# Two FNet + gated-unit layers on one core: a new hand-written opening, and input tests moved away from layer 2's first down projection

## The chip, the core and the metric

One core of one Trainium2 chip runs the kernel. TensorE (PE) does the matrix products, VectorE (DVE) and ScalarE (ACT) the elementwise work, GpSimd (POOL) small work, and SyncE (SP) issues the loads and stores. The metric is the device time of one execution in microseconds (us).

## The reference

The input x has 2048 rows (sequence) of 640 columns (hidden). Two layers follow, with the same weights, each of two residual steps:

```python
def _A_ref(x, dft_seq_re, dft_seq_im, dft_hid_re, dft_hid_im):
    a = jnp.einsum("bsd,ed->bse", x, dft_hid_re)
    b = jnp.einsum("bsd,ed->bse", x, dft_hid_im)
    return jnp.einsum("ts,bse->bte", dft_seq_re, a) - jnp.einsum("ts,bse->bte", dft_seq_im, b)

def _B_ref(x, w_gate, w_up, w_down):
    h = _sigmoid(x @ w_gate) * (x @ w_up)        # 640 -> 1728
    return h @ w_down                            # 1728 -> 640

for layer in range(2):
    x = x + _A_ref(_layernorm(x), ...)
    x = x + _B_ref(_layernorm(x), ...)
```

All arrays are float32. The four DFT matrices are inputs like the others: 2048 x 2048 for the sequence, 640 x 640 for the hidden dimension, real and imaginary part each.

## The kernel before

**Two programs in one.** `folded` does the work under the assumption that the DFT matrices have the symmetries of a DFT; it folds rows and columns onto each other, so that a quarter of the sequence matrix is enough, and makes the gate, up and down products from seven block products instead of eight. Operands are split into a high and a low float16 part. At the same time it tests on the chip whether the matrices do have those symmetries, and writes the result to `flag`. If they don't, `general` computes everything again in the plain way; on the inputs given it does not run.

**The tests.** There are 100. Each loads a piece of a DFT matrix (`load_rows`, L1490, four loads; `load_hidden_rows`, L1550, two loads that gather single rows; and their like for columns), compares it with its mirror image on VectorE (L1497 and L1499, L1554), and sums the squares of what is left on ScalarE (L1469). Three rooms of memory are used in turn. Test n's load is placed at `at_test(n)`, its compares at `at_test(n + 2)`, its square just after, at `n + 2.85`. All loads stand in SP's queue, together with those that the layers need.

**Order by a plan.** The program is straight-line code, and each engine works off its own queue in the order in which it was written. From the end of the opening on the order comes from a plan: the list of TensorE's steps with estimated durations gives each a place on an axis T of about one unit per us, and `when(t, f)` writes job f at place t of that axis, between the steps. It sets an order only; nothing waits for a clock. `start_of(1, "d", 0)`, here called d0, is the place of layer 2's (layer index 1) first down projection. The tests are spread evenly over a list of stretches with weights, `spans`: a stretch of weight 0.4 has tests at 0.4 of the density of one with weight 1.0, and `pace` is the weighted sum of the lengths divided by 100.

**The down projection.** Layer 2's down runs in seven stages (`stage`, L1418) for each half of the columns. Each stage needs three tables of 320 KB each, which layer 1 had stored in HBM as `kept_f`; `load_stage(s)` (L1366) loads them. Stage 0's are placed at d0 - 16, stage 1's at d0 + 0.5, stage 2's at d0 + 5. The results are taken out of the accumulators by VectorE (L1292). The products ahead of it, gate and up, are `seven` (L1162); ScalarE copies their accumulators out (L1166). Behind the down comes the next gate and up, whose input is turned by a transposing load (L528).

**The opening.** For the first part of layer 1, up to the first gate and up, the order of the jobs is a string written by hand, `OPENING`. A row block i is 512 rows, in four parts A to D of 128. `turn i B` mirrors a part on TensorE (L352), `turned` copies the result out on ScalarE (L358). `stats i A` takes the statistics of a part for the layer norm: on ScalarE (L578, L579) when `(i, GA)` is in `ON_ACT`, on VectorE (L419, L420) otherwise. `col i k` folds columns of two parts (L588, L589, twice VectorE), `double` is L595 on GpSimd, `zero i` clears the columns past the fold (L846, GpSimd). `means`, `smeans`, `power` and `scale` work out the norm's factors (L375, L363, L400/L401, L405 to L409), `re`, `ro`, `de`, `do` scale the folded rows (ScalarE L629 and L631, VectorE L635), `join i e` and `join i o` add them up (L665), and `seq` is the first product on TensorE (L824). `evhi` and `ev` take its result out as a high (L237, ScalarE) and a low part (L239, VectorE). Loads of weights (`wld`) and splits (`whhi`, `wshi` and so on) stand between.

**Memory.** All big buffers are slots of one tile, `big`. Which address a slot gets is read from a long list of numbers, `PLACES`, in the order in which the slots are taken; a changed order needs a new list.

Of the kernel before, what the change touches and what calls it, by code (L numbers as in the profile page):

```python
# [19 lines left out]
D = 640  # L20
# [50 lines left out]
JC = 6  # L71
# [35 lines left out]
311 372 252 359 204 297 350 151 264 212 377 100 226 132 161 118 355"""  # L107
# [20 lines left out]
class Slot:  # L128
# [19 lines left out]
GA, GB, GC, GD = range(4)  # L148
# [13 lines left out]
    smeans 2, means 2, turn 3 C, ro 1 0, join 0 e, ro 1 1, double 1 1, re 1 1, do 0 1, do 1 0, power 2, double 2 0,
    re 1 0, join 0 o, turned 3 C, turned 3 B, do 1 1, stats 3 A, square 3 C, zero 1, square 3 B, de 1 1, scale 2,
    de 1 0, join 1 o, seq 0 1, ro 2 0, row 1, stats 3 D, means 3, re 2 0, join 1 e, col 3 1, col 3 0, double 2 1,
    ro 2 1, smeans 3, seq 0 0, de 2 0, re 2 1, power 3, do 2 0, do 2 1, seq 1 1, de 2 1, double 3 0, seq 1 0,
    double 3 1, evhi 0 1 2, ev 0 1 2, wshi 1 0, whhi 1, scale 3, evhi 0 1 1, ro 3 1, join 2 e, join 2 o, wld 4 1,
    re 3 1, evhi 0 1 0, re 3 0, whhi 3, de 3 1, do 3 1, ro 3 0, de 3 0, seq 2 0, do 3 0, whhi 4, join 3 e, join 3 o,
    ev 0 1 1, evhi 0 0 0, wld 5 0, evhi 0 0 2, whhi 2, zero 3, whhi 5, seq 3 0, ev 0 0 0, whlo 5, wshi 3 0,
    evhi 1 0 0, evhi 0 0 1, whhi 0, ev 1 0 0, wld 3 1, seq 2 1, evhi 1 0 1, ev 0 0 2, ev 0 0 1, wshi 2 1, whlo 1,
    whlo 3, whlo 0, whlo 2, wshi 4 1, wshi 1 1, whlo 4, ev 1 0 1, wshi 0 0, hid 0 0, evhi 1 0 2, ev 1 0 2, wslo 1 1,  # L170
    hid 0 1, wslo 2 1, difhi 0, ev 0 1 0, difhi 1, wslo 3 0, dif 0, dif 1, seq 3 1, evhi 1 1 1, hid 1 1, wshi 0 1,
# [8 lines left out]
ON_ACT = {(0, GA), (2, GA), (2, GD), (3, GA), (3, GD)}  # L180
# [22 lines left out]
def folded(ctx, tc, pool, dram, big, acc, flag, x, ct, wh, wg, wu, wc, wd, out):  # L203
# [1509 lines left out]
    def start_of(*key):  # L1713
        return T[marks[key]]
# [83 lines left out]
    for layer in range(2):  # L1798
# [343 lines left out]
```

## Time and profile before

| | us |
|---|---|
| median of 3 runs | 1116.61 |
| the three runs | 1118.42, 1116.54, 1116.61 |
| profiled execution, its own time | 1118.15 |
| its span, first to last instruction | 1116.3 |
| mean granted TensorE clock | 0.992 |
| TensorE busy | 1090.2 (98%) |
| VectorE busy | 827.8 (74%) |
| ScalarE busy | 570.8 (51%) |
| GpSimd busy | 157.6 (14%) |

Rows of the profile that stand below come in four forms. A row of the order of time has the start in us, the duration in us, the engine, the line of the program, the operation, what it writes and reads, and how often it came in a row; in square brackets stands how long the engine sat idle before it and what ended that. "SPq" is SyncE issuing a load. A row of the waits has the engine and its line, what it waited for, and us in total, times and longest. A row of the windows gives busy time by engine and the granted clock (PEclk, 1.00 is full), the DMA share and GB/s. "big<-kept_f" means that `big` is written from `kept_f`; in the windows (x72) is a count of instructions.

### The profile page before, as it was taken

The numbers are of one execution on the slowest core, as the hardware profiler recorded it, in microseconds if no ns is written. First come the engines' busy times: TensorE is split into PE (matmuls) and PEld (weight loads), VectorE is DVE, ScalarE is ACT, GpSimd is POOL, SyncE is SP. The second block draws the span as 40 slices with busy tenths as digits, with TensorE's granted clock in tenths as the row PEclk, the third lists the DMA queues.
The fourth block names the chain that finished last, engine by engine and source line by source line (L and its number), as shares of the span: only waits on it lengthen the run. The fifth ranks groups of instructions, "written<-read, shape, count | busy, mean of one in ns | idle before, by whom it ended". The sixth has DMA issues, their size and how long they took to land.

```text
span 1116.3 us, 17439 instructions
## 1 busy us (share of the span) xinstructions
PE 1090.2 (98%) x6279; PEld 620.7 (56%) x6279; DVE 827.8 (74%) x1608; ACT 570.8 (51%) x1108; POOL 157.6 (14%) x245
## 2 busy tenths in 40 slices
PE   5999999999999999999999999999999999999997
PEld 3667444447774444457776844444567444444775
DVE  7986679857548999769786559876797356767962
ACT  7765447765334656455234534575554245454520
POOL 3110143321324143000100100002000010000010
PEclk8899999999999999999999999999999999999999
DMA  8414674365888789656733049635669875665621
GB/s 272 151 37 106 180 208 170 100 214 153 206 232 274 252 228 281 212 171 218 220 90 112 1 88 169 208 120 188 200 150 196 219 228 188 207 207 175 201 84 63
DMA packets 183081, 194.70 MB, mean 174 GB/s; under 512 B 76459, under 2 KB 145476, under 8 KB 182984
## 3 DMA queue, kind: packets, MB, share of 16 engines
q1 hardware_dynamic: 182344, 190.86, 58.4%
q0 software_dynamic: 640, 2.62, 0.6%
q8 instruction: 51, 0.84, 0.3%
q14 instruction: 46, 0.38, 0.1%
HBM read 145.29 MB, written 31.90 MB: 159 GB/s over the span
## 4 chain that ended last, share of the span: by engine, by line
PE 86%; DVE 7%; DMA 5%; ACT 1%; issue 1%; SPq 0%; DVEq 0%; POOL 0%; ACTq 0%; POOLq 0%
PE acc L1162 37%; PE acc L1418 14%; PE acc L1118 14%; PE acc L1304 8%; PE acc L912 4%; DMA big<-in_ct 2%; PE acc L824 2%; PE acc L1399 2%; PE acc L1271 2%; PE acc L781 1%; DMA big<-big 1%; DMA big<-in_x 1%; DVE big L1292 1%; DVE big L239 1%; DVE big L1379 0%
## 5 line engine op out<-in xcount | busy, mean ns | idle before, releaser
L1162 PE MATMUL acc<-big 128*128 128x512 f16 x2160 | 467.8, 379 | 2.8 <-DMA big<-big 1.1
L1162 PEld LDWEIGHTS <-big 128*128 128x128 f16 x2160 | 211.2, 98 | 258.1 <-issue 3.0
L1418 PE MATMUL acc<-big 128*128 128x320 f16 x1512 | 214.0, 299 | 5.1 <-DVE big L1292 2.5
L1418 PEld LDWEIGHTS <-big 128*128 128x128 f16 x1512 | 147.8, 98 | 64.3 <-issue 4.0
L1166 ACT ACTIVATE big<-acc 128x512 f32<-128x512 f32 x160 | 93.8, 592 | 168.6 <-PE acc L1162 168.2
L1118 PE MATMUL acc<-big 128*128 128x512 f16 (+1 forms) x900 | 156.3, 336 | 0.0
L1118 PEld LDWEIGHTS <-big 128*128 128x128 f16 x900 | 87.9, 98 | 67.6 <-issue 0.3
L1469 ACT ACTIVATE big<-big 128x768 f32<-128x768 f32 (+6 forms) x106 | 79.1, 746 | 85.2 <-DVE big L1499 43.9
L239 DVE SCALAR_TENSOR_TENSOR big<-big 128x640 f16<-128x640 f32 (+8 forms) x94 | 75.8, 831 | 22.6 <-POOL big L1072 11.4
L1304 PE MATMUL acc<-big 128*128 128x320 f16 x656 | 89.3, 299 | 0.0
L1292 DVE SCALAR_TENSOR_TENSOR big<-acc,big 128x320 f32<-128x320 f32 x112 | 53.0, 484 | 47.6 <-PE acc L1399 27.3
L1379 DVE TENSOR_TENSOR big<-big 128x512 f16<-128x512 f32 x126 | 84.5, 681 | 4.5 <-ACT big L1378 4.4
L237 ACT ACTIVATE big<-big 128x640 f16<-128x640 f32 (+9 forms) x94 | 63.6, 708 | 43.2 <-DMA big<-in_ct 19.6
L1378 ACT ACTIVATE big<-big 128x512 f16<-128x512 f32 x126 | 72.6, 616 | 18.6 <-DVE big L1379 7.0
L1304 PEld LDWEIGHTS <-big 128*128 128x128 f16 x656 | 64.2, 98 | 25.1
L1212 DVE TENSOR_TENSOR big<-big,acc 128x512 f32<-128x512 f32 x40 | 27.2, 681 | 42.6 <-PE acc L1162 32.0
L1169 ACT ACTIVATE big<-big 128x512 f32<-128x512 f32 x80 | 49.7, 621 | 9.9 <-DVE big L1212 6.8
L381 POOL DMA_INDIRECT out<-big,rows x8 | 9.1, 1140 | 313.0 <-DVE big L1292 168.8
L1497 DVE TENSOR_TENSOR big<-big 128x512 f32<-128x512 f32 x64 | 44.9, 702 | 10.3 <-DMA big<-in_ct 10.1
L511 ACT ACTIVATE big<-big 128x384 f16<-128x384 f32 (+2 forms) x56 | 36.2, 667 | 31.0 <-DVE big L496 18.8
L1390 DVE TENSOR_TENSOR big<-big 128x512 f32<-128x512 f32 x72 | 50.2, 699 | 0.1
L512 DVE TENSOR_TENSOR big<-big 128x384 f16<-128x384 f32 (+2 forms) x56 | 42.6, 774 | 8.4 <-ACT big L511 8.4
(193 smaller groups left out, 1199.1 us busy)
## 6 DMA issues: line engine op xcount, KB each, us to landing
big<-in_ct SPq DMA_DIRECT2D x256, 128.0 KB
big<-kept_f SPq DMA_DIRECT2D x63, 320.0 KB
big<-kept_S SPq DMA_DIRECT2D x33, 512.0 KB
big<-kept_w SPq DMA_DIRECT2D x33, 320.0 KB
big<-in_ct SPq DMA_DIRECT2D x32, 256.0 KB
big<-kept_G SPq DMA_DIRECT2D x21, 320.0 KB
kept_S<-big SPq DMA_DIRECT2D x13, 512.0 KB
big<-in_wg SPq DMA_DIRECT2D x19, 320.0 KB
```

Of the source, the lines that this page charges most:

```text
L237: nc.scalar.activation(dh, src, AF.Copy, scale=s)
L239: nc.vector.scalar_tensor_tensor(dl, src, s, dh, op0=OP.mult, op1=OP.subtract)
L1118: nc.tensor.matmul(ps, w[wp][:, d * P : (d + 1) * P], xt[:, xp, :], start=(d == 0 and wp == HI and xp == HI), stop=(d == ND - 1 and wp == LO))
L1162: nc.tensor.matmul(ps, wt, xt, start=start and n == 0, stop=n == len(todo) - 1, skip_group_check=not start)
L1166: nc.scalar.activation(dst, ps, AF.Copy)
L1292: nc.vector.scalar_tensor_tensor(xe, ps[:, :EH], CB, xe, op0=OP.mult, op1=OP.add)
L1304: nc.tensor.matmul(held["pd", i, e][0][:, :EH], held["t", half, j].parts[hp][:, i * P : (i + 1) * P], held["w", 2, j].parts[wp][:, e * EH ...
L1378: nc.scalar.activation(h, v, AF.Copy)
L1379: nc.vector.tensor_tensor(l, v, h, op=OP.subtract)
L1390: nc.vector.tensor_tensor(o, a, b, op=op)
L1418: nc.tensor.matmul(ps[:, :EH], a[n][hp][:, i * P : (i + 1) * P], w[n][:, wp], start=fresh and m == 0, stop=m == len(todo) - 1, skip_group_ ...
L1469: nc.scalar.activation(v, v, AF.Square, accum_out=new_sum()[:p])
```

## The change

It has four parts.

1. `ON_ACT` holds (0, GD) in place of (0, GA): of the first row block, part A's statistics are now taken on VectorE, and part D's on ScalarE.
2. `OPENING` is written in another order. `zero 0` and `zero 1` stand ahead of `col 0 0`; `stats 0 A` stands right behind `turned 0 B`; `ev 0 0 2` stands ahead of `de 3 1`, `seq 2 0`, `do 3 0` and `join 3 e`; the weight loads come as 5 0, 4 0, 3 0 in place of 4 0, 3 0, 4 1 and so on.
3. `spans`: the stretch ahead of d0 ends 7 units before it, and the one behind goes from d0 + 6 to d0 + 58 with weight 0.45 in place of d0 to the next gate and up (79 units) with weight 0.4. The weighted sum gets smaller, so `pace` goes from 4.61 to 4.45 units for all tests.
4. `PLACES` is a new list throughout.

```diff
@@ OPENING, first and some later lines
-    turn 0 B, wld 4 0, stats 0 A, turned 0 B, turn 0 C, turn 1 B, square 0 B, turned 0 C, stats 0 D, col 0 0,
-    square 0 C, wld 3 0, means 0, col 0 1, smeans 0, turned 1 B, double 0 0, square 1 B, turn 1 C, zero 0, turn 2 B,
-    stats 1 D, turned 1 C, double 0 1, square 1 C, power 0, turn 2 C, col 1 0, turned 2 B, stats 1 A, means 1,
+    turn 0 B, turned 0 B, stats 0 A, wld 5 0, turn 0 C, square 0 B, turned 0 C, turn 1 B, zero 0, zero 1, col 0 0,
+    stats 0 D, square 0 C, col 0 1, turn 1 C, turned 1 B, wld 4 0, double 0 1, square 1 B, stats 1 A, stats 1 D,
+    means 0, smeans 0, power 0, turn 2 B, turned 1 C, square 1 C, turned 2 B, double 0 0, means 1, col 1 0,
...
-    re 3 1, evhi 0 1 0, re 3 0, whhi 3, de 3 1, do 3 1, ro 3 0, de 3 0, seq 2 0, do 3 0, whhi 4, join 3 e, join 3 o,
+    evhi 0 0 2, join 2 e, re 3 1, ro 3 0, de 3 0, evhi 0 1 1, whhi 4, whhi 1, whhi 0, do 3 1, ev 0 0 2, de 3 1,
+    seq 2 0, do 3 0, evhi 0 0 0, join 3 e, evhi 0 0 1, join 3 o, seq 3 0, whhi 2, ev 0 0 0, wld 5 1, whlo 0, whlo 2,
...
-ON_ACT = {(0, GA), (2, GA), (2, GD), (3, GA), (3, GD)}
+ON_ACT = {(0, GD), (2, GA), (2, GD), (3, GA), (3, GD)}
...
-             (start_of(1, "c", 1, 0) + 5, start_of(1, "j", 0, JC), 0.7), (start_of(1, "j", 0, JC), start_of(1, "d", 0), 1.0),
-             (start_of(1, "d", 0), start_of(1, "j", 1, 0), 0.4),
+             (start_of(1, "c", 1, 0) + 5, start_of(1, "j", 0, JC), 0.7), (start_of(1, "j", 0, JC), start_of(1, "d", 0) - 7, 1.0),
+             (start_of(1, "d", 0) + 6, start_of(1, "d", 0) + 58, 0.45),
```

The first statistics and column folds on VectorE, before; `quad` holds a row block's statistics, "waits" names the semaphores that the instruction waits for (DMAHW: a load, Activation: ScalarE, Pool: GpSimd):

```order
L419 BN_STATS quad_74<-big 128x6 [waits DMAHW3_49]
L419 BN_STATS quad_74<-big 128x6
L420 BN_AGGR quad_74<-quad_74 128x2 [waits DVE_49]
L588 TENSOR_TENSOR big<-big 128x2x320 [waits DMAHW1_49,Activation_49]
L589 TENSOR_TENSOR big<-big 128x2x320
L588 TENSOR_TENSOR big<-big 128x2x320 [waits Activation_49]
L589 TENSOR_TENSOR big<-big 128x2x320
L375 TENSOR_SCALAR quad_74<-quad_74 128x3 [waits Activation_49]
L419 BN_STATS quad_75<-big 128x6 [waits DMAHW5_49,DMAHW4_49,DMAHW3_49]
L419 BN_STATS quad_75<-big 128x6
L420 BN_AGGR quad_75<-quad_75 128x2 [waits DVE_49]
```

And after:

```order
L419 BN_STATS quad_74<-big 128x6 [waits DMAHW1_49]
L419 BN_STATS quad_74<-big 128x6
L420 BN_AGGR quad_74<-quad_74 128x2 [waits DVE_49]
L588 TENSOR_TENSOR big<-big 128x2x320 [waits Activation_49]
L589 TENSOR_TENSOR big<-big 128x2x320
L588 TENSOR_TENSOR big<-big 128x2x320 [waits DMAHW3_49,Activation_49]
L589 TENSOR_TENSOR big<-big 128x2x320 [waits Pool_49]
L419 BN_STATS quad_75<-big 128x6 [waits DMAHW2_49]
L419 BN_STATS quad_75<-big 128x6
L420 BN_AGGR quad_75<-quad_75 128x2 [waits DVE_49]
L419 BN_STATS quad_75<-big 128x6 [waits DMAHW5_49,DMAHW4_49,DMAHW3_49]
```

The statistics ahead wait for another load, a second set of statistics of row block 1 has moved up, and the fourth column operation waits for GpSimd.

GpSimd in the same place, behind its long first instruction, before:

```order
L244 MEMSET wmax 128x42
L248 ISA
L248 IOTA rows 128x1 x4
L249 IOTA rows 1x1 [waits Pool_49]
L248 IOTA rows 128x1 x4
L249 IOTA rows 1x1 [waits Pool_49]
L363 TENSOR_SCALAR quad_74<-quad_74 128x3 [waits Activation_49]
L595 TENSOR_SCALAR big<-big 128x2 [waits DMAHW1_49,DVE_49]
L846 MEMSET big 128x2 [waits DVE_49]
L595 TENSOR_SCALAR big<-big 128x2 [waits DMAHW3_49]
L401 TENSOR_TENSOR quad_74<-quad_74,minus 128x4 [waits DVE_49]
```

And after:

```order
L244 MEMSET wmax 128x42
L248 ISA
L248 IOTA rows 128x1 x4
L249 IOTA rows 1x1 [waits Pool_49]
L248 IOTA rows 128x1 x4
L249 IOTA rows 1x1 [waits Pool_49]
L846 MEMSET big 128x2 x2
L595 TENSOR_SCALAR big<-big 128x2 [waits DMAHW3_49,DVE_49]
L363 TENSOR_SCALAR quad_74<-quad_74 128x3 [waits Activation_49]
L401 TENSOR_TENSOR quad_74<-quad_74,minus 128x4 [waits DVE_49]
L595 TENSOR_SCALAR big<-big 128x2 [waits DMAHW1_49]
```

The memsets of L846 stood behind VectorE's work and waited for it; now they stand right behind the address rows (L248, L249) and wait for nothing, and VectorE waits for them.

SyncE around layer 2's first down, before; the first L1366 group holds stage 0's tables, the second stage 1's, `kept_w` (L1046) are the down's remaining weights:

```order
L1490 DMA big<-in_ct 128x1x256 x4
L1366 DMA big<-kept_f 128x1280 x3
L1550 DMA big<-in_wh 128x1x320 x2
L1046 DMA big<-kept_w_12_2350 128x1280
L1046 DMA big<-kept_w_13_2364 128x1280
L1490 DMA big<-in_ct 128x1x256 x8
L1366 DMA big<-kept_f 128x1280 x3
L1490 DMA big<-in_ct 128x1x256 x4
L1366 DMA big<-kept_f 128x1280 x6
L1550 DMA big<-in_wh 128x1x320 x2
L1366 DMA big<-kept_f 128x1280 x3
```

And after:

```order
L1060 DMA big<-kept_tw 128x512
L1550 DMA big<-in_wh 128x1x320 x2
L1490 DMA big<-in_ct 128x1x256 x4
L1366 DMA big<-kept_f 128x1280 x3
L1490 DMA big<-in_ct 128x1x256 x4
L1046 DMA big<-kept_w_12_2350 128x1280
L1046 DMA big<-kept_w_13_2364 128x1280
L1490 DMA big<-in_ct 128x1x256 x4
L1366 DMA big<-kept_f 128x1280 x9
L1550 DMA big<-in_wh 128x1x320 x2
L1490 DMA big<-in_ct 128x1x256 x4
```

Stages 1, 2 and 3 now have their nine tables in a row, with four test loads between the L1046 pair and them in place of eight; the pair of L1550 loads that stood ahead of the L1046 pair stands further up.

More of the change, by code (lines that the diff above doesn't have):

```diff
@@ L74 @@
 PLACES = """
[32 rows of a table removed]
-311 372 252 359 204 297 350 151 264 212 377 100 226 132 161 118 355"""
[32 rows of a table added]
+161 201 319 333 344 358 301 354 235 196 309 315 182 130 107 378 297"""
 class Slots:
@@ L156 @@
 OPENING = """
-    turn 0 B, wld 4 0, stats 0 A, turned 0 B, turn 0 C, turn 1 B, square 0 B, turned 0 C, stats 0 D, col 0 0,
-    square 0 C, wld 3 0, means 0, col 0 1, smeans 0, turned 1 B, double 0 0, square 1 B, turn 1 C, zero 0, turn 2 B,
-    stats 1 D, turned 1 C, double 0 1, square 1 C, power 0, turn 2 C, col 1 0, turned 2 B, stats 1 A, means 1,
-    smeans 1, scale 0, double 1 0, stats 2 A, re 0 0, re 0 1, power 1, turned 2 C, ro 0 1, ro 0 0, stats 2 D,
-    col 1 1, square 2 B, turn 3 B, col 2 0, de 0 1, scale 1, square 2 C, de 0 0, do 0 0, col 2 1, row 0, zero 2,
@@ L162 @@
[L162 to L166, printed above, removed]
@@ L167 @@
-    re 3 1, evhi 0 1 0, re 3 0, whhi 3, de 3 1, do 3 1, ro 3 0, de 3 0, seq 2 0, do 3 0, whhi 4, join 3 e, join 3 o,
[L168 to L171, printed above, removed]
@@ L172 @@
-    sum 0, wshi 3 1, add 0, nst 1, evhi 1 1 0, ev 1 1 1, nst 0, sum 1, npow 0, add 1, hid 2 0, hidev 2 0, ev 1 1 0,
-    nscale 0, hidev 1 1, cmb 1 1, nrm 0, nst 2, nrm 1, nst 3, npow 1, evhi 1 1 2, hid 3 0, nhi 1, ev 1 1 2, hid 1 0,
-    wslo 0 1, hid 2 1, nlo 1, nscale 1, hidev 3 0, wshi 2 0, wld 5 1, nrm 2, nhi 0, hid 3 1, hidev 2 1, nlo 0,
-    hidev 1 0, nrm 3, nhi 3, tp 0, nhi 2, wslo 1 0, wslo 0 0, tpl 0, nlo 3, wshi 4 0, tp 1, mid, tph 0, nlo 2, tp 3,
-    hidev 3 1, tp 2, cmb 1 0, tph 1, tpl 1, wslo 2 0, jn 1 0, tph 3, midhi, gu 1 0, jn 1 1, tpl 3, middif, tph 2,
@@ new lines @@
+    means 0, smeans 0, power 0, turn 2 B, turned 1 C, square 1 C, turned 2 B, double 0 0, means 1, col 1 0,
+    stats 2 D, col 1 1, smeans 1, turn 2 C, scale 0, zero 2, re 0 0, col 2 0, turned 2 C, ro 0 0, power 1, re 0 1,
+    double 1 0, de 0 0, col 2 1, turn 3 B, scale 1, square 2 C, ro 0 1, wld 3 0, turn 3 C, do 0 1, de 0 1,
+    square 2 B, do 0 0, stats 2 A, double 1 1, ro 1 1, double 2 0, join 0 e, re 1 0, ro 1 0, re 1 1, join 0 o,
+    smeans 2, means 2, do 1 1, turned 3 C, turned 3 B, stats 3 A, do 1 0, zero 3, square 3 C, seq 0 1, square 3 B,
@@ new lines @@
+    power 2, stats 3 D, de 1 0, de 1 1, join 1 o, scale 2, ro 2 0, join 1 e, row 0, double 2 1, col 3 1, means 3,
+    col 3 0, double 3 1, seq 0 0, seq 1 1, re 2 1, ro 2 1, smeans 3, power 3, do 2 0, row 1, seq 1 0, wld 4 1,
+    de 2 1, re 2 0, do 2 1, evhi 0 1 0, evhi 0 1 2, double 3 0, scale 3, de 2 0, ro 3 1, join 2 o, whhi 5, re 3 0,
+    evhi 0 0 2, join 2 e, re 3 1, ro 3 0, de 3 0, evhi 0 1 1, whhi 4, whhi 1, whhi 0, do 3 1, ev 0 0 2, de 3 1,
+    seq 2 0, do 3 0, evhi 0 0 0, join 3 e, evhi 0 0 1, join 3 o, seq 3 0, whhi 2, ev 0 0 0, wld 5 1, whlo 0, whlo 2,
@@ new lines @@
+    ev 0 0 1, whhi 3, whlo 1, whlo 3, whlo 5, evhi 1 0 1, whlo 4, evhi 1 0 0, ev 1 0 0, hid 0 0, wshi 2 1,
+    evhi 1 0 2, ev 1 0 1, wshi 1 0, ev 1 0 2, ev 0 1 1, hid 0 1, ev 0 1 0, ev 0 1 2, difhi 0, seq 2 1, difhi 1,
+    dif 0, dif 1, sum 0, wshi 3 0, add 0, wshi 4 0, nst 1, seq 3 1, nst 0, sum 1, npow 0, add 1, wshi 4 1,
+    evhi 1 1 1, evhi 1 1 0, wld 3 1, wshi 1 1, ev 1 1 1, nscale 0, hid 1 0, nst 2, wshi 0 0, nrm 1, nst 3, hid 1 1,
+    wshi 0 1, evhi 1 1 2, nrm 0, mid, nhi 0, ev 1 1 0, hidev 1 1, npow 1, wshi 2 0, nhi 1, wslo 1 0, ev 1 1 2, nlo 0,
@@ new lines @@
+    wshi 3 1, hidev 1 0, hid 3 0, midhi, nscale 1, tp 0, tpl 0, nlo 1, nrm 3, nhi 3, wslo 1 1, hidev 3 0, hid 2 1,
+    tph 0, middif, nlo 3, wslo 0 0, tp 1, cmb 1 0, tp 3, tph 1, tpl 1, hid 2 0, nrm 2, cmb 1 1, tph 3, hidev 2 0,
+    wslo 0 1, jn 1 0, gu 1 0, nhi 2, nlo 2, tp 2, ad 1 0, tpl 3, tph 2, hid 3 1, jn 1 1, tpl 2, ad 1 1, wslo 4 0,
+    wslo 3 1, pst 2, wslo 4 1, pst 1, gu 1 1, gu 0 0, pst 3, pst 0, wslo 2 0, psc 1, wslo 2 1, ap 2, ap 0, hidev 2 1,
+    hidev 3 1, gu 0 1, ap 3, ap 1, wslo 3 0, pp 1, pp 3, pp 0, gu 2 0, ptr 0, pp 2, ptr 2, ptr 3, gu 2 1, ptr 1"""
```

2 lines of the change are left out of this document (removed), and 64 rows, old and new, of the table PLACES.

## The prediction

> **What bounds the kernel now.** I read the page's engine shares first, then what TensorE waited for, then the windows and the order of time at the two places that the change touches.
>
> ```profile
> span 1116.3 us, 17439 instructions
> PE 1090.2 (98%) x6279; PEld 620.7 (56%) x6279; DVE 827.8 (74%) x1608; ACT 570.8 (51%) x1108; POOL 157.6 (14%) x245
> ```
>
> TensorE sets the end: 1116.3 - 1090.2 = 26.1 us of idle is all that a new order can win at most, since no matmul is added or taken. The waits of TensorE (total, times, longest) say where a part of it lies:
>
> ```profile
> PE twin L352 <- DVE big L308: 4.1, 1, 4.1
> PE acc L824 <- POOL quad L363: 3.6, 1, 3.6
> PE acc L1418 <- DVE big L1292: 2.5, 4, 1.2
> PE acc L1418 <- DMA big<-kept_f: 2.5, 2, 2.3
> ...
> PE acc L1162 <- DMA big<-big: 1.1, 1, 1.1
> PE acc L1162 <- ACT big L1166: 1.0, 1, 1.0
> ```
>
> L352 and L824 are the opening; L1418 is the down projection in the form that layer 2 uses. The stretch at layer 2's first down, on all engines:
>
> ```profile
> 777.45 1.94 SPq L1550 DMA_DIRECT2D big<-in_wh  x2
> 779.44 4.18 SPq L1046 DMA_DIRECT2D big<-kept_w  x2
> 783.72 8.92 SPq L1490 DMA_DIRECT2D big<-in_ct  x8
> 786.58 9.94 PE L1418 MATMUL acc<-big 128*128 128x320 f16 x72
> 790.30 0.49 DVE L1554 TENSOR_TENSOR big<-big 128x320 f32<-128x320 f32 x1 [4.85 <-DMA big<-in_ct]
> 790.88 0.47 ACT L1469 ACTIVATE big<-big 128x320 f32<-128x320 f32 x1 [4.73 <-DVE big L1554]
> 792.73 1.52 SPq L1366 DMA_DIRECT2D big<-kept_f  x3
> 798.82 2.11 PE L1418 MATMUL acc<-big 128*128 128x320 f16 x12 [2.30 <-DMA big<-kept_f]
> 815.80 2.60 PE L1418 MATMUL acc<-big 128*128 128x320 f16 x18 [1.23 <-DVE big L1292]
> 818.85 3.42 PE L1418 MATMUL acc<-big 128*128 128x320 f16 x24 [0.45 <-DVE big L1292]
> ```
>
> TensorE ran stage 0 of the down to 786.58 + 9.94 = 796.5 and then stood until stage 1's three tables of 320 KB had landed at 798.8, 6.1 us after their issue. They were issued late because SP was 8.92 us over eight test loads (1.1 us each). At the same time VectorE stood 4.85 us and ScalarE 4.73 us at the head of their queues for the slow pair of test loads issued at 777.45. Some 18 us later TensorE waits twice for VectorE (1.23 + 0.45):
>
> ```profile
> core 0: us, PE busy (x) PEld busy (x) DVE busy (x) ACT busy (x) POOL busy (x), PEclk, DMA share, GB/s
> 780.00:800.00 20.00, 17.55 (x111) 10.53 (x109) 12.56 (x23) 8.29 (x16) 0.00 (x0) 1.00 0.57 184
> 800.00:820.00 20.00, 18.16 (x131) 12.72 (x131) 19.27 (x38) 15.41 (x29) 0.00 (x0) 1.00 0.61 191
> ```
>
> VectorE is at 63% and then at 96%: what it could not do while it stood, it catches up when the down needs it. The two stretches lack 2.45 + 1.84 = 4.3 us of TensorE, and this is the prize.
>
> **The change, part by part: the tests.** The number of tests stays at 100, and so does their arithmetic; their places move. Around layer 2's first down 13 units of the plan are now without a test, those ahead of it stand closer (4.45 units apart instead of 4.61 in the spans of weight 1), those behind it at weight 0.45 instead of 0.4.
>
> (1) Stage 1's load. Between the second L1046 load and these tables stand four test loads instead of eight, and the L1550 pair that stood just ahead of the L1046 pair now stands eleven loads ahead of it. Four issues at 1.1 us are 4.5 us: the tables go out at 788.3 and land 6.1 us later at 794.4, some 2.1 us before TensorE needs them. So the kept_f waits go: -2.5 us. Nothing gets late in its place, since the next two stages' tables now follow at once (nine in a row). The bounds are 0 (SP held by something else) and -2.5.
>
> (2) The waits for L1292. VectorE no longer stands for the L1550 pair right there, and 4.85 us is well over 1.23 + 0.45. But the tests that were due at about 799 and 811 stay near 800 and 809, and VectorE's 96% there stays. I take -1.2 of the 1.7, nearer to the full sum since the stand is three times the wait; bounds 0 and -1.7.
>
> (3) The transposed load behind the down:
>
> ```profile
> 858.79 9.90 SPq L528 DMA_TRANSPOSE big<-big  x1
> 872.27 2.97 PE L1162 MATMUL acc<-big 128*128 128x512 f16 x13 [1.10 <-DMA big<-big]
> ```
>
> From d0 + 58 on there is no test for 21 units, so fewer test loads stand in the queue about 850 to 866. The transpose needs 13.4 us from its issue to TensorE's start anyway. I take -0.5, half of 1.10; bounds 0 and -1.1.
>
> (4) The tests that had to go stand elsewhere, 3% closer. They cost TensorE nothing as long as a test's ACT square and DVE compares fit into idle time: ScalarE is busy 51%, VectorE 74%. If the cover is gone, it is the second rival below. Taken 0.
>
> **The opening.** Its rows, on VectorE, GpSimd, ScalarE and TensorE, and the granted clock:
>
> ```profile
> 8.45 0.89 DVE L419 BATCH_NORM_STATS2 quad<-big 128x6 f32<-128x320 f32 x2 [3.49 <-DMA big<-in_x]
> 11.67 0.82 DVE L589 TENSOR_TENSOR big<-big 128x640 f32<-128x640 f32 x1
> 12.13 0.37 POOL L248 IOTA rows<- 128x1 int32 x4 [11.04 <-issue]
> 13.34 0.09 POOL L846 MEMSET big<- 128x2 f32 x1
> 13.41 0.89 DVE L419 BATCH_NORM_STATS2 quad<-big 128x6 f32<-128x320 f32 x2 [0.85 <-DMA big<-in_x]
> 25.18 0.88 DVE L665 TENSOR_TENSOR big<-big 128x321 f32<-128x321 f32 x2
> 26.16 1.19 PE L824 MATMUL acc<-big 128*128 128x256 f32 x2 [3.60 <-POOL quad L363]
> 27.25 0.88 DVE L665 TENSOR_TENSOR big<-big 128x320 f32<-128x320 f32 x2
> 28.05 1.00 DVE L635 SCALAR_TENSOR_TENSOR big<-big,quad 128x320 f32<-128x320 f32 x2
> 28.18 2.08 PE L824 MATMUL acc<-big 128*128 128x256 f32 x4 [0.83 <-DVE big L665]
> 43.65 6.51 PE L824 MATMUL acc<-big 128*128 128x256 f32 x28
> 44.27 1.69 DVE L665 TENSOR_TENSOR big<-big 128x321 f32<-128x321 f32 x4
> 47.54 1.09 ACT L237 ACTIVATE big<-acc 128x512 f16<-128x512 f32 x2 [1.18 <-PE acc L824]
> 48.18 1.89 DVE L239 SCALAR_TENSOR_TENSOR big<-acc,big 128x512 f16<-128x512 f32 x3 [0.62 <-ACT big L237]
> 20.00:33.50 13.50, 9.01 (x19) 5.47 (x20) 13.22 (x38) 11.75 (x29) 4.03 (x8) 0.50 0.89 274
> 33.70:40.00 6.30, 6.30 (x27) 4.32 (x27) 4.58 (x11) 4.43 (x10) 3.11 (x8) 1.00 0.90 348
> ```
>
> (5) The statistics of part A on VectorE run inside its 3.49 us of idle before 8.45 and cost nothing; those of part D (0.89 and a short L420) leave VectorE for ScalarE, which gives up A's in return. VectorE so comes to L588 about 1 us earlier, at about 8.45.
>
> (6) A new wait takes this back. `zero 0` and `zero 1` (L846 on GpSimd) now stand ahead of `col 0 0` in the order, so the fourth L588/L589 operation waits for both. GpSimd does nothing before 12.13 and came to L846 at 13.34, behind L363 and L595, which now stand behind it; two memsets of 0.09 end at about 13.1. VectorE, through with three operations of 0.82 at about 10.9, stands 2.1 us; before it stood 0.85 us ahead of 13.41. Queued behind it are the statistics 1 A and 1 D, and by way of `power 0` all that leads to the first joins (L665).
>
> (7) What of this reaches TensorE? Its unbroken run starts with `join 0 o`, which ends at 28.13, after a first pair that waited for `join 0 e` (26.06; the page names L363, which was long done). Before, VectorE worked almost without a break from 13.41 to the end of `join 0 e`. Now it starts at 13.1 (0.3 earlier), with that L589 (0.82) and one more L635 (`do 0 1`, 0.50) ahead of `join 0 e`: 26.06 - 0.3 + 0.8 + 0.5 = 27.1, and `join 0 o` now follows it closely, ending 0.9 later at 28.0. The first pair starts 1.0 us later, the 0.83 us wait goes, the run starts as before. Taken 0; bounds -0.8 (only that wait goes) and +2.1 (the whole stand reaches TensorE).
>
> (8) Between the last matmuls of `seq 1 0` and `seq 2 0` the new order puts `ev 0 0 2` ahead of `de 3 1`, `do 3 0` and both joins of row block 3. From TensorE's end: L237 0.55, L239 0.63, two L635 of about 0.50, two L665 at 0.42 are 3.0 us, against `seq 2 0`'s 12 matmuls at 0.23 = 2.8. The wait is 0.24; the second join's two operations follow 0.84 later against two matmuls (0.46): some 0.36 more. In all +0.6, bounds 0 and +1.2.
>
> **Sum.** -2.5 - 1.2 - 0.5 + 0 + 0 + 0.6 = -3.6 us, from the profiled execution's own 1118.15 us to 1114.55. That execution lies 1.54 above the median of 1116.61, so against the median 1113.0.
>
> **Rivals.** *SP stays the bound.* [...] If the four loads that left are replaced by waiting for those now ahead, the tables land at 798.8 as before, and (1) and (2) give nothing: 1118.15 - 0.5 + 0.6 - 1.54 = 1116.7, no change. [...]
>
> *Slower: ScalarE held by a test.* A test's square (L1469) stands in ScalarE's queue until VectorE has compared, and that until the load has landed; behind it wait the copies (L1166) that free TensorE's accumulators.
>
> ```profile
>   DVE big L1499: 43.9, 11
> ```
>
> This row lists what ScalarE sat idle for ahead of L1469: 11 times, 43.9 us. Before, only 1.0 us of TensorE's idle came from L1166, and none between 700 and 786. If the closer tests ahead of the down meet such a copy, each costs 4.73 less the cover of one nine-matmul group (9 x 0.216, as L1162 in layer 2 shows with 2.97 us for 13: 2.1), so 2.6 us. It decides from 5.8 us on, thus with three of them: 1113.0 + 7.8 = 1120.8.
>
> *The clock in the opening.* It was 0.50 to 33.5 us and 1.00 behind, with TensorE unbroken from 28.18. If it is granted as early as the run begins, TensorE wins (33.6 - 28.2)/2 = 2.7 us: 1110.3. If it comes as much later, it loses 2.7: 1115.7. For it speaks that (6) to (8) shift TensorE's first work by up to 1.0 us; against it that the run starts at the same time. [...]
>
> **Numbers.** A measurement of this kernel can tell about 0.2%, 2.2 us. Forecast 0.48, SP stays the bound 0.18, ScalarE held 0.18, clock 0.16 (half each way). The forecast's own range is 1111.3 to 1114.6 (all of the prizes; or (2) and (3) without gain). Faster: 0.46 of the forecast and 0.08 of the clock, 0.54. Same: 0.18 + 0.08 + 0.02 = 0.28. Slower: 0.18. The range reaches down to the early clock, 1110.2, and up past SP's case and one or two held copies, 1118.4; three held copies are left out.
>
> **What would show it.** After: kept_f gone from TensorE's waits and the tables of stage 1 issued by about 789 (step 1); L1292's total for L1418 down from 2.5 to about 1.3 (2); L528's wait under 1.1 (3); no L1166 entry above 1.0 (4). In the opening a VectorE row near 13.1 with some 2 us of idle released by GpSimd (6), one pair of L824 at about 27.1 without the 0.83 wait (7), and two short waits of L824 for L665 near 47 us (8). I am wrong if stage 1's tables still land after TensorE asks, if waits in layer 1 or at 700 to 786 appear that were not there, or if full clock starts at another time than 33.6.

## The result, and the profile after

The changed kernel takes 1112.84 us (median of 7, 1110.59 to 1114.74) against 1118.62 us for the kernel before on the same chip (median of 7, 1116.54 to 1121.29). The ratio is 0.9947, 95% interval 0.9933 to 0.9962: 5.9 us faster, within 4.2 to 7.5. The forecast was 1113.0 us, a step of 3.6. The profiled execution of the changed kernel took 1114.74 us, the longest of its seven, 3.41 less than the profiled one before. One execution of the kernel before in a later round took 2329.47 us, about twice as long; it is left out of the ratios, and its cause is not known.

The page's engine shares and the waits of TensorE (line, what it waited for, us in total, times, longest):

```profile
span 1112.9 us, 17458 instructions
PE 1086.5 (98%) x6279; PEld 619.0 (56%) x6279; DVE 828.0 (74%) x1608; ACT 571.1 (51%) x1108; POOL 153.7 (14%) x245
```

```profile
PE acc L824 <- issue: 4.6, 1, 4.6
...
PE acc L1162 <- ACT big L1166: 2.5, 2, 2.2
PE acc L1162 <- DMA big<-in_ct: 1.6, 1, 1.6
...
PE acc L1418 <- DVE big L1292: 0.8, 2, 0.4
```

The waits for kept_f and for the transposed load are gone, and L1292's fell from 2.5 to 0.8. A wait that was 1.0 before is now 2.5 (L1166), and one of 1.6 is new. The same places in the order of time, SyncE and TensorE near layer 2's first down:

```profile
785.69 3.44 SPq L1490 DMA_DIRECT2D big<-in_ct  x4
788.83 12.39 PE L1418 MATMUL acc<-big 128*128 128x320 f16 x90
789.41 10.54 SPq L1366 DMA_DIRECT2D big<-kept_f  x9
816.53 17.27 PE L1418 MATMUL acc<-big 128*128 128x320 f16 x126 [0.37 <-DVE big L1292]
868.69 11.60 PE L1162 MATMUL acc<-big 128*128 128x512 f16 x53
```

The tables of stage 1 go out 0.6 us after the down has begun (789.41 - 788.83; before 792.73 - 786.58 = 6.15), TensorE runs 90 matmuls without a gap, and of the two L1292 waits behind, 0.37 us is left. But the down itself starts at 788.83, later than the 786.58 of before. The loss lies in layer 1, here in the changed kernel:

```profile
334.94 2.62 SPq L1490 DMA_DIRECT2D big<-in_ct  x4
337.67 0.41 SPq L1330 DMA_DIRECT2D big<-in_wd  x1
343.48 1.00 ACT L237 ACTIVATE big<-big 128x960 f16<-128x960 f32 x1 [4.49 <-DMA big<-in_wd]
344.39 0.58 ACT L1166 ACTIVATE big<-acc 128x512 f32<-128x512 f32 x1
345.02 1.44 PE L1162 MATMUL acc<-big 128*128 128x512 f16 x3 [2.19 <-ACT big L1166]
```

A test's four loads (L1490) now go out ahead of three weight loads (`in_wd`: L1330, L1331, L1328). ScalarE waits 4.49 us for the weights with L237, and behind that stands the copy L1166 that frees TensorE's accumulator. The windows show a second price, the granted clock (third column from the end):

```profile
344.00:346.00 2.00, 0.98 (x3) 0.41 (x3) 1.97 (x5) 2.00 (x5) 1.92 (x3) 0.73 0.68 225
346.00:348.00 2.00, 2.00 (x7) 0.65 (x5) 2.00 (x4) 1.52 (x2) 0.22 (x1) 0.50 0.55 182
```

Behind the wait the clock was half for about 3.4 us (344.9 to 348.3). A second profile of the same kernel (below) has the wait and not the half clock.

Since TensorE does the same matmuls, the place of the time can be read exactly: the start of the same matmul in two traces, called a mark below. The table gives how much each stretch of the program gained (-) or lost against the first profile of the kernel before; its second profile shows how far this moves by itself. The columns run from the change to parts of it.

| stretch, by the times of before | before again | changed | changed again | spans alone | opening alone | changed, weights first |
|---|---|---|---|---|---|---|
| opening, to 88 us | -0.4 | -1.4 | -1.1 | +0.2 | -1.1 | -1.3 |
| 88 to 263 | -0.7 | -0.9 | -1.2 | -0.7 | -1.2 | -1.2 |
| 263 to 371 | +1.1 | +4.9 | +2.3 | +1.0 | +0.3 | +0.1 |
| 371 to 770 | 0.0 | -0.6 | -0.6 | -0.6 | 0.0 | -0.7 |
| layer 2's first down, 770 to 822 | +0.5 | -4.3 | -5.1 | -5.1 | +1.1 | -5.1 |
| 822 to 880 | -0.6 | -1.3 | -1.3 | -1.3 | -0.9 | -1.3 |
| all, to 880 us | -0.1 | -3.6 | -7.0 | -6.4 | -1.8 | -9.4 |

### The profile page after: what moved, and what is told of

It reads as the page before. It is cut to its first block, busy times and chain, and to the rows that moved or that the text cites. A ratio compares the mean times of both kernels' runs of the same rounds, so it can differ in the third digit from the quotient of the medians.

```text
span 1112.9 us, 17458 instructions
## 1 busy us (share of the span) xinstructions
PE 1086.5 (98%) x6279; PEld 619.0 (56%) x6279; DVE 828.0 (74%) x1608; ACT 571.1 (51%) x1108; POOL 153.7 (14%) x245
## 4 chain that ended last, share of the span: by engine, by line
PE 83%; DVE 7%; DMA 3%; ACT 2%; issue 2%; SPq 2%; POOL 1%; DVEq 0%; POOLq 0%; ACTq 0%
PE acc L1162 37%; PE acc L1418 15%; PE acc L1118 14%; PE acc L912 4%; PE acc L1304 4%; PE acc L1399 2%; PE acc L824 2%; PE acc L1271 2%; PE acc L781 1%; SPq L528 1%; DMA big<-in_wh 1%; DMA big<-in_wu 1%; DVE big L239 1%; DVE big L1379 1%; DVE big L512 0%
## 5 line engine op out<-in xcount | busy, mean ns | idle before, releaser
L1166 ACT ACTIVATE big<-acc 128x512 f32<-128x512 f32 x160 | 94.0, 592 | 178.7 <-PE acc L1162 176.1
L1469 ACT ACTIVATE big<-big 128x768 f32<-128x768 f32 (+6 forms) x106 | 79.0, 746 | 67.6 <-DVE big L1499 24.1
L239 DVE SCALAR_TENSOR_TENSOR big<-big 128x640 f16<-128x640 f32 (+7 forms) x94 | 77.2, 844 | 23.9 <-ACT big L237 23.8
L237 ACT ACTIVATE big<-big 128x640 f16<-128x640 f32 (+9 forms) x94 | 63.8, 707 | 54.7 <-DMA big<-in_ct 20.2
L1292 DVE SCALAR_TENSOR_TENSOR big<-acc,big 128x320 f32<-128x320 f32 x112 | 53.1, 485 | 47.2 <-PE acc L1399 26.0
L1497 DVE TENSOR_TENSOR big<-big 128x512 f32<-128x512 f32 x64 | 45.4, 709 | 6.8 <-DMA big<-in_ct 6.6
```

The costliest lines, as they stand in the source:

```text
L237: nc.scalar.activation(dh, src, AF.Copy, scale=s)
L239: nc.vector.scalar_tensor_tensor(dl, src, s, dh, op0=OP.mult, op1=OP.subtract)
L1166: nc.scalar.activation(dst, ps, AF.Copy)
L1292: nc.vector.scalar_tensor_tensor(xe, ps[:, :EH], CB, xe, op0=OP.mult, op1=OP.add)
L1469: nc.scalar.activation(v, v, AF.Square, accum_out=new_sum()[:p])
```

## The experiments

**Parts of the change.** The two halves come apart cleanly: the new spans with the old opening, and the other way round, each with the list of addresses that goes with its opening.

```diff
 spans_only, against the kernel before:
-             ... (start_of(1, "j", 0, JC), start_of(1, "d", 0), 1.0),
-             (start_of(1, "d", 0), start_of(1, "j", 1, 0), 0.4),
+             ... (start_of(1, "j", 0, JC), start_of(1, "d", 0) - 7, 1.0),
+             (start_of(1, "d", 0) + 6, start_of(1, "d", 0) + 58, 0.45),
 opening_only: OPENING, ON_ACT and PLACES as in the change, these lines as before
```

> The new spans alone; opening, ON_ACT and the addresses as before. Theory: the two parts of the change add up. Against the kernel before, the profiles gave -4.6 us at layer 2's first down (TensorE's waits for kept_f and L1292), -1.3 at the transposed load behind it, and +4.8 at 336 to 350 us, where one test's four loads now stand ahead of three weight loads (in_wd): so about -1 us, ratio 0.999, and a TensorE wait for ScalarE's L1166 of about 2 us near 346. Rival: that stretch in layer 1 was chance of one execution, and then -5.9 us, ratio 0.995, without that wait.

> The new opening, ON_ACT and the new list of addresses alone; spans as before. Theory: -1.4 us in the opening (first unbroken L824 run 1.3 us earlier, clock 0.7, the two waits near 47 us +0.5) and -0.9 at 219 us, so -2.3 us, ratio 0.998; the waits for kept_f (about 2.5) and L1292 (about 2.5) near 800 stay. Rival: the opening is worth nothing but the clock's chance, so 0 +- 1.7 us, ratio 0.9985 to 1.0015. Second rival: the new addresses carry part of the gain, so that the waits near 800 get shorter here too.

The spans alone give 1111.97 us, ratio 0.9960 (0.9947 to 0.9973); the opening alone 1117.02 us, ratio 1.0004 (0.9995 to 1.0013). So nearly all of the gain is the spans'. The wait in layer 1 came with them, as the theory had it, but at 1.70 us and without the half clock:

```profile
344.61 15.70 PE L1162 MATMUL acc<-big 128*128 128x512 f16 x72 [1.70 <-ACT big L1166]
```

With the opening alone the waits at the down stand as before, so the new addresses are not what removed them:

```profile
797.10 0.99 PE L1418 MATMUL acc<-big 128*128 128x320 f16 x6 [2.53 <-DMA big<-kept_f]
814.97 2.60 PE L1418 MATMUL acc<-big 128*128 128x320 f16 x18 [0.71 <-DVE big L1292]
798.00:804.00 6.00, 5.80 (x31) 3.49 (x30) 5.47 (x12) 3.56 (x7) 0.00 (x0) 0.72 1.01 305
```

In that execution the wait for kept_f was followed by half clock (0.72 over 6 us).

**The kernels again.** Nothing is edited.

> The changed kernel once more, for a second profile. Theory: the wait for L1166 near 345 us follows from the order of the loads, so it stands here again, 2.2 us within 0.7, followed by a stretch at half clock, and the time is 1113 us. Rival: a load that came late by chance in one execution; then it is gone here. The opening's half clock may begin at another time; the GpSimd rows that came at 10.7 instead of 12.1 us tell whether that start moves by itself.

> The kernel before once more: a second profile, and how far a ratio moves with no change at all. Theory: ratio 1.000 within 0.001. Profile: the waits for kept_f (2 to 2.7) and L1292 (1.7) near 800 again, since they follow from the order of loads; in the opening a first pair of L824 at 25.8 to 26.7, the unbroken run 2.0 us behind it; the wait for the transposed load near 872 anywhere from 0.2 to 1.2. Rival: the waits near 800 differ by more than 1 us, and what was read from single profiles was chance.

The changed kernel: 1111.05 us, ratio 0.9947 (0.9934 to 0.9960), the L1166 wait there again with 1.89 us, no half clock behind it. The kernel before: ratio 1.0000 (0.9987 to 1.0013), with the same waits:

```profile
11.14 0.37 POOL L248 IOTA rows<- 128x1 int32 x4 [10.06 <-issue]
798.82 0.99 PE L1418 MATMUL acc<-big 128*128 128x320 f16 x6 [2.31 <-DMA big<-kept_f]
816.29 2.60 PE L1418 MATMUL acc<-big 128*128 128x320 f16 x18 [1.65 <-DVE big L1292]
```

GpSimd's first row of L248, at 12.13 in the first profile, stands at 11.14 here. Over the 14 profiles it lies between 10.43 and 12.13.

**The loss in layer 1.** One number puts the weight loads ahead of that test's loads again.

```diff
-    spans = [..., (start_of(0, "d", 0) + 76, start_of(0, "e"), 0.55),
+    spans = [..., (start_of(0, "d", 0) + 77, start_of(0, "e"), 0.55),
```

> The changed kernel with the tests' second span starting at 77 instead of 76 units, so that the three weight loads (in_wd) stand ahead of that test's four loads again, as in the kernel before. Theory: TensorE's 2.2 us for L1166 at 345 us and the half clock behind it (1.3) go, so -3.5 us against the changed kernel, ratio 0.992 to the kernel before (1109.5 us). Rival: TensorE is bound there by the transposed load (1.6 us), the gain is given back, and the time stays at 1113.

> The changed kernel with the weight loads ahead of the test's loads, a second time: whether it stays ahead of the changed kernel. Theory: ratio 0.9935 within 0.0008, and no wait for L1166 near 345 us in its profile.

1109.31 us, ratio 0.9935 (0.9921 to 0.9949); the second time 1110.36 us, 0.9939 (0.9920 to 0.9958). The wait for L1166 is gone in both profiles; what is left at that place is short:

```profile
335.90 24.33 PE L1162 MATMUL acc<-big 128*128 128x512 f16 x112 [0.79 <-DVE big L1292]
```

Its two ratios are the lowest of all kernels tried. Against the changed kernel it gained 1.7 us by the medians of the same round, 0.9 by the second ratio; the intervals overlap, so that the wait is gone is shown, and the size of the gain is not. It is less than the 3.5 expected: that sum had counted the half clock as if it came every time, and the profiles have it once in five executions with that wait.

**What held the tables at the down.** Two edits of the kernel before keep the number of tests and leave no hole. The first moves the slow pair away; eight test loads stay ahead of stage 1's tables.

```diff
+    tests[52], tests[54] = tests[54], tests[52]
```

> The kernel before, with two tests exchanged in the list: the hidden-rows test whose two slow loads (L1550) went out at 777 us, nine ahead of layer 2's first down, changes places with a rows test two places earlier, so it goes out some 9 us sooner. The number of test loads ahead of stage 1's tables stays eight. Theory A (SP is held by the slow loads, the eighth load back in the queue, and so is VectorE): SP loses its 2.6 us of standing, stage 1's tables go out about 790, the wait for kept_f falls from 2.5 to under 0.5 and that for L1292 behind it from 1.7 to under 0.6: -3.5 us, ratio 0.997. Theory B (as the prediction counted, it is the number of loads): kept_f stays at 2 us or more, time as before.

```profile
784.24 7.07 SPq L1490 DMA_DIRECT2D big<-in_ct  x8
791.40 2.88 SPq L1366 DMA_DIRECT2D big<-kept_f  x3
788.70 12.39 PE L1418 MATMUL acc<-big 128*128 128x320 f16 x90
814.81 2.60 PE L1418 MATMUL acc<-big 128*128 128x320 f16 x18 [1.23 <-DVE big L1292]
778.58 5.10 PE L1271 MATMUL acc<-big 128*128 128x512 f16 x15 [2.23 <-DMA big<-kept_w]
```

The wait for kept_f is gone, as theory A has it, and the tables go out 2.7 us after the down's start instead of 6.15. But that is TensorE's lateness and not SP's haste: TensorE waits 2.23 us for kept_w at 778, with half clock behind it (0.86 over the 12 us to 788.70). Counted from the same matmul (at 770.17 before, 768.21 here) the down starts 4.1 us later than before and the tables go out 0.6 us later. So this run shows no gain for SP, and decides neither theory. The waits for L1292 stayed as they were, 1.23 and 0.45, although VectorE no longer stood at the down's start (the first ten us of the down, before and here; VectorE is the fifth and sixth figure, 5.47 and 9.00 us busy):

```profile
786.58:796.58 10.00, 9.94 (x73) 6.95 (x71) 5.47 (x10) 4.08 (x8) 0.00 (x0) 1.00 0.55 178
```

```profile
788.70:798.70 10.00, 10.00 (x75) 7.23 (x74) 9.00 (x17) 5.07 (x10) 0.00 (x0) 1.00 0.68 213
```

In all 1118.67 us, ratio 1.0019 (1.0009 to 1.0030). What the pair does to SP stands in SP's own waits, in the kernel before, here, and in the run of the second edit below:

```profile
SPq L1490 <- DMA big<-in_wh: 2.6, 1, 2.6
SPq L1366 <- DMA big<-in_wh: 2.4, 1, 2.4
SPq L1366 <- DMA big<-in_wh: 2.8, 1, 2.8
```

In the kernel before SP stands 2.6 us among the eight test loads until the pair has landed; here it stands 2.4 us for it further ahead, at stage 0's tables. The second edit moves one test's four loads behind the tables and leaves the slow pair.

```diff
-        when(at_test(n), within, n % 3, load, *key)
+        when(at_test(n) + (5.0 if n == 56 else 0.0), within, n % 3, load, *key)
```

> The kernel before, with the loads of a single test (four, due at 672.2 on the plan) put five units later, so that they stand behind stage 1's three tables; everything else in place, the slow L1550 pair too. The prediction's count (four issues fewer): tables out about 788 to 790, wait for kept_f from 2.5 to under 0.5, while VectorE still stands for the slow pair, so the waits for L1292 (1.7 near 816 to 819) stay: -2 us, ratio 0.998. If those L1292 waits came from TensorE's late start instead, they go too: -4. If the slow pair holds SP as well, the tables go out after 790 all the same and kept_f keeps 1 us or more.

```profile
787.82 4.86 SPq L1366 DMA_DIRECT2D big<-kept_f  x3
791.36 0.49 DVE L1554 TENSOR_TENSOR big<-big 128x320 f32<-128x320 f32 x1 [5.18 <-DMA big<-kept_f]
798.18 0.97 PE L1418 MATMUL acc<-big 128*128 128x320 f16 x6 [0.27 <-DMA big<-kept_f]
812.74 2.60 PE L1418 MATMUL acc<-big 128*128 128x320 f16 x18 [2.27 <-DVE big L1292]
817.00 2.60 PE L1418 MATMUL acc<-big 128*128 128x320 f16 x18 [1.66 <-DVE big L1292]
```

With four loads fewer ahead the first table goes out 5.4 us sooner, counted from the same matmul as above, the third 2.0. The wait for kept_f falls from 2.5 to 0.55, as counted; but VectorE stands 5.18 us for the pair (the row names another load, but L1554 compares the pair's rows), and the waits for L1292 rise from 1.7 to 2.27 + 1.66 + 0.45 = 4.4. The ratio is 1.0011 (0.9998 to 1.0023), no gain. None of the three expectations was right on this point: with the tables on time, VectorE is the next bound.

VectorE's compares for tests (L1497, L1499, L1554), added up over the first 26 us of the down, are 2.9 us before, 3.4 with the slow pair moved, 2.9 with one test's loads moved, 1.2 in the changed kernel. TensorE's L1292 waits there are 1.7, 1.7, 4.4 and 0.4 us.

**The opening.** Three edits of the changed kernel, the first on top of the weights first.

```diff
 zero_on_vector:
-        nc.gpsimd.memset(o[:, GB::2, EH:], 0.0)
+        (nc.vector if i < 2 else nc.gpsimd).memset(o[:, GB::2, EH:], 0.0)
 zero_columns_late:
-    ... turn 1 B, zero 0, zero 1, col 0 0, stats 0 D, square 0 C, col 0 1,
+    ... turn 1 B, col 0 0, stats 0 D, square 0 C, col 0 1, zero 0, zero 1,
 stats_on_act_again:
-ON_ACT = {(0, GD), (2, GA), ...
+ON_ACT = {(0, GA), (2, GA), ...
```

> The changed kernel with the weight loads first (second span from 77) and, new, the two memsets of row blocks 0 and 1 (L846) on VectorE instead of GpSimd, so that nothing in the opening waits for GpSimd's late start. Theory: VectorE's stand of 1.7 us behind L588 goes for 0.2 us of memsets; TensorE's unbroken L824 run starts at about 25 instead of 26.05 to 26.5, so -1 us in the opening (the clock adds up to 1.7 either way) and 1108.3 us, ratio 0.9926. Rival: the chain into L824 is set by the last rows of x or by ScalarE, VectorE just waits elsewhere, and the run starts at 26 as before.

> The changed kernel with zero 0 and zero 1 written behind col 0 1 instead of ahead of col 0 0; GpSimd's memsets then wait for VectorE. Theory (the fourth L588/L589 operation starts with the later of GpSimd's memsets and the third operation, and 13.7 us lie from its end to the first L824): VectorE waits for GpSimd nowhere ahead of 13 us, and TensorE's run starts 13.7 us behind that operation's end; if the third operation ends by 10 us, as in the changed kernel's first profile, the run starts at about 24.5 instead of 26.05, otherwise at 26 to 26.8 as with the memsets on VectorE. Rival: a later step (power 0 through GpSimd) holds the joins, and the distance grows to 15 us.

> The changed kernel with part A's statistics of the first rows on ScalarE and part D's on VectorE, as in the kernel before; the order of the opening stays new. Theory (step 5 of the prediction, the exchange frees VectorE by 0.9 us after 8.45): the fourth L588/L589 operation comes 0.5 to 1.1 us later than with the exchange whenever the rows are there, the run starts at 26.8 to 27.5: +0.7 us, ratio 0.9955. Rival: VectorE stands for rows or GpSimd anyway, the exchange costs nothing, run at 26.0 to 26.8.

The changed kernel itself, the third and fourth column operation, GpSimd's first row behind the memsets of its first us, and TensorE's run:

```profile
9.11 0.83 DVE L588 TENSOR_TENSOR big<-big 128x640 f32<-128x640 f32 x1
11.60 0.84 DVE L589 TENSOR_TENSOR big<-big 128x640 f32<-128x640 f32 x1 [1.66 <-POOL big L846]
10.71 0.37 POOL L248 IOTA rows<- 128x1 int32 x4 [9.63 <-issue]
26.05 11.11 PE L824 MATMUL acc<-big 128*128 128x256 f32 x38 [4.60 <-issue]
```

With the memsets on VectorE:

```profile
10.85 0.83 DVE L588 TENSOR_TENSOR big<-big 128x640 f32<-128x640 f32 x1 [1.81 <-ACT big L358]
26.83 11.47 PE L824 MATMUL acc<-big 128*128 128x256 f32 x38 [5.05 <-issue]
```

With the memsets written late:

```profile
9.86 0.82 DVE L589 TENSOR_TENSOR big<-big 128x640 f32<-128x640 f32 x1
11.71 0.89 DVE L419 BATCH_NORM_STATS2 quad<-big 128x6 f32<-128x320 f32 x2 [1.03 <-DMA big<-in_x]
25.60 11.56 PE L824 MATMUL acc<-big 128*128 128x256 f32 x38 [4.43 <-DVE big L665]
```

With part A's statistics on ScalarE:

```profile
11.58 0.85 DVE L589 TENSOR_TENSOR big<-big 128x640 f32<-128x640 f32 x1
26.05 10.30 PE L824 MATMUL acc<-big 128*128 128x256 f32 x38 [3.45 <-issue]
```

Without the wait for GpSimd another wait stands there: for the copy out of the turned rows (1.81 us) in the first, which two profiles with the memsets on GpSimd have too (1.78 and 2.51), and for the next rows of x (1.03) in the second. The run starts at 26.83 and 25.60, the second only 0.45 ahead of 26.05: there 14.9 us lie from the end of the fourth operation to the run instead of 13.6, the distance that the rival had named. Times and ratios are 1110.05 us, 0.9942 (0.9930 to 0.9954); 1111.91 us, 0.9948 (0.9929 to 0.9966); and 1113.24 us, 0.9955 (0.9940 to 0.9971). None is apart from the kernel that it was edited from, 0.9935 and 0.9939 for the first, 0.9947 for the others. With the exchange of statistics undone the fourth operation comes at 11.58 all the same, when GpSimd's memsets are done. By the marks at 88 us the three lie at -0.3, -1.4 and -2.2 us.

At last the old opening with the new spans and the weights first, so that only the opening differs from the best kernel:

> The opening, ON_ACT and addresses of the kernel before; the new spans with the weight loads first (second span from 77). Against in_wd_first (ratio 0.9935) it differs in the opening alone. Theory (opening worth 1.1 to 1.8 us by the marks of four profiles): ratio 0.9947 and the unbroken L824 run at 28.2. Rival (opening worth nothing, as the time of opening_only said): ratio 0.9935.

1110.30 us, ratio 0.9940 (0.9927 to 0.9953), beside 0.9935 and 0.9939: the rival's side. The opening's worth is not to be told from nothing by the times. By the marks at 88 us, the five profiles with the whole new opening lie at -0.9 to -1.4 (mean -1.2), the six with the old one at +0.2 to -1.2 (mean -0.2).

## Why the prediction was right, and where its steps were not

The time, its side and its range were right, and the forecast's case is the one that came: the waits at the down are gone. But the single terms were partly luck, and so is the time: the step was 5.9 us where 3.6 was forecast, and 1112.84 lies beside 1113.0 because the kernel before came out at 1118.62, 2.0 above the median of three that the forecast started from.

**The bound of 26.1 us.** The prediction took TensorE's idle for all that a new order can win. It isn't: at half clock the same matmuls are busy for longer (L352 in the kernel before: eight in 2.39 us at 14.01 with the clock at 1.00, four in 2.50 at 20.06 with 0.50). In the first pair of profiles the idle stayed (26.1 and 26.4 us) and the busy time fell by 3.7 (1090.2 to 1086.5); in the second pair the idle fell by 4.0 and the busy time by 2.7 (1088.4 to 1085.7). Most of the busy time won lies ahead of 88 us, where the clock changes several times: in the first pair TensorE is busy for 76.4 us there at a mean clock of 0.92 before, and up to the same mark for 71.9 us at 0.96 in the changed kernel.

**(1) kept_f, taken -2.5.** It went, in all nine profiles with the new spans. The reason was half right. The prediction counted eight issues of 1.1 us; but in 2.6 of the 8.92 us SP stood for the slow pair. Four loads fewer alone brought the first table from 6.15 to 0.8 us behind the down's start, but the second and third then waited for the pair's landing (issued 787.82, 791.33 and 792.35). Both held SP. In the changed kernel SP stands as long for the pair, but it is through with it 8 us ahead of the down.

**(2) L1292, taken -1.2.** The size was right (-1.3 in the changed kernel, -1.7 in others), the reason is not borne out. The prediction gave the 1.7 us to VectorE's stand for the slow pair; but with the stand moved ahead of the down they stayed at 1.7, even with TensorE 4.1 us later. With the stand in place and the tables on time they are 4.4. By these two executions the stand is worth 2.7 us, and in the kernel before SP's lateness of 2.5 covered it. The 1.7 that show may go with the tests' compares during the down, of which the hole takes 1.7 us away as well (2.9 to 1.2); that fits the four profiles, but no run moved the compares alone, so it is not shown. Terms (1) and (2) are not two prizes that add: taking only SP's lateness away moved the time by nothing. The change takes loads, stand and compares out of this place at once; what each is worth alone stays open. The stretch as a whole gave -4.3 to -5.1 where 3.7 was summed.

**(3) The transposed load, taken -0.5.** No wait for L528 is left behind the down in any profile with the new spans, against 0.17 to 1.24 us with the old. The stretch gave -1.3 against the first profile; the five with the old spans lie there at +0.1 to -0.9, so some 1.0 us is the usual gain.

**(4) Tests elsewhere, taken 0.** This is the step that failed. It cost 1.6 to 2.2 us at 344, once with the half clock behind it. The price of the rival was near (2.6 for a held L1166), its mechanism and place were not: no square L1469 in the way and not the dense stretch ahead of the down, but three weight loads pushed behind four test loads in SP's queue, by a shift of 0.8 units of the plan in a loose stretch (weight 0.55). The order of SP's queue showed that; I had compared it at the down only.

**(5) and (6), the opening's VectorE.** The wait for GpSimd came as counted in kind (1.66 us here, 0 to 2.27 in the other executions), and the exchange of statistics proved worth nothing, since GpSimd or the rows set the fourth operation. **(7) taken 0.** The forecast had TensorE's run start as before, at 28.2. It starts 14.45 us behind the start of the fourth column operation in six of the eight profiles with the new opening. Had GpSimd begun at 12.13 as in the profile I read, that would be 13.1 + 14.45 = 27.5, near the 27.1 forecast for the first pair; it began at 10.4 to 11.3 and the run at 25.8 to 26.7. One execution's start of an engine was taken for a fixed number. **(8) taken +0.6.** Right: the marks lose 0.5 us in the changed kernel between two matmuls at 42.6 and 45.4, and TensorE's weight loads show for whom:

```profile
45.39 2.06 PEld L824 LDWEIGHTS acc<-big 128*128 128x128 f32 x10 [0.49 <-DVE big L665]
```

By marks the opening gained about 1 us where +0.6 was summed, by the times nothing. The bounds of (7) and (8) together, -0.8 to +3.3, hold the second and just miss the first. Whether later waits give that us back was not settled; the waits for the transposed load and L1292 near 336 us, 0.3 to 1.8 in these traces, are a candidate.

**The rivals.** SP as the bound fell with (1). The clock case came in part: the last change to full clock in the opening lies between 29.2 and 34.0 us in the 14 profiles, on average at 31.1 with the whole new opening and 33.1 with the old, which by the prediction's own reckoning (half of it) is 1.0 us. Nor was it half all the time before: in the first profile of the kernel before it was full from 13.1 to 19.9 us, in that of the changed one from 7.0 to 24.1. One sum is slightly off and changes nothing: 9 x 0.216 is 1.9, which makes a held copy 2.8 us.

That the sum of -3.6 and the profiled pair's -3.4 agree is chance. The stretch from 263 to 371 us lost 4.9 us in that execution, and the other stretches won 4.9 us beyond the sum: 0.6 at the down, 0.8 behind it, 2.0 in the opening, 1.5 in the two stretches for which nothing was summed (of which the second profile of before has 0.7 too). The seven executions show the usual gain, 5.9.

## What to carry to other kernels

When work is taken out of one place and spread over others, compare the order of the queues over the whole program: what matters is which load now stands ahead of which, and a shift by less than a unit in a loose stretch can cost as much as the dense one that was feared (1.6 to 2.2 us here, where 2.6 was feared). Two waits that end one behind the other on the same engine are not two prizes: the first hides the second, and removing one alone may show no gain (here kept_f's wait fell from 2.5 to 0.55 us and L1292's rose from 1.7 to 4.4, ratio 1.0011). A load's place should be counted from a matmul that both traces share: its distance from another engine's start shrinks as well when that engine comes late. A start time of an engine that waits for nothing in the profile should be read from more than one execution before a sum rests on it (GpSimd's lay between 10.43 and 12.13 us).

## What the runs showed of the hardware

**Half clock behind short waits.** Seven waits of TensorE of 2.2 to 2.6 us stand in the 14 traces behind the opening. Three were followed by about 3.4 us of granted clock 0.50 (2.19 at 345, 2.53 at 797, 2.23 at 778), a further loss of about 1.7 us each, an estimate: half of the 3.4 us; four were not (2.30, 2.31, 2.21, 2.27). The length of the wait does not tell them apart: 2.19 us had the half clock behind it and 2.31 did not. The changed kernel around 345 us, then the kernel before around 798 us (the second figure is TensorE's busy time, the third from the end the clock):

```profile
341.50:344.91 3.41, 1.33 (x7) 0.49 (x5) 1.43 (x2) 1.43 (x3) 2.18 (x3) 1.00 0.94 319
344.91:348.32 3.41, 3.30 (x8) 1.17 (x8) 3.34 (x9) 2.61 (x5) 1.23 (x2) 0.50 0.55 188
794.76:798.18 3.42, 1.76 (x13) 1.04 (x11) 3.32 (x8) 1.67 (x3) 0.00 (x0) 1.00 0.85 285
798.18:801.59 3.41, 2.46 (x16) 1.55 (x17) 3.25 (x7) 2.50 (x5) 0.00 (x0) 1.00 0.92 237
```

In the 3.41 us up to the first half clock TensorE was busy for 1.33 us. Around the second wait it was busy for 1.76 of 3.42 us and then for 2.46 of 3.41, and the clock stayed at 1.00. No run set the length or the place of such a wait alone, so what decides whether the half clock follows is not shown.

**GpSimd's first row of L248** began between 10.43 and 12.13 us in 14 profiles, 9.35 to 11.04 us after its first memsets, in which the profile shows nothing to wait for.

**A pair of loads held two queues.** The last L1550 pair ahead of the down held SP for 2.4 to 2.8 us and VectorE for 4.6 to 6.0 us in all 14 profiles, in the kernel before (2.6 and 4.85) as in the changed one (2.6 and 6.02). What differs is where it does so: until 3.7 us behind the down's start before, until 7.9 us ahead of it after. It is not the kind of load alone: of 10 such compares in a profile two or three waited for more than 1.5 us, all between 720 and 792 us.
